# Clustered attention with a gated output block, one core: low parts of k and q by accumulating transfers, key tiles of two more pairs summed ahead of TensorE

## The chip, the cores and the metric

One core of one Trainium2 chip. The metric is the time of one execution on the device in microseconds (us), the median of several runs. An engine works through its own queue of instructions in order; engines wait for each other by semaphores. Names of engines: PE is TensorE, DVE is VectorE, ACT is ScalarE, POOL is GpSimd, SP is SyncE, which issues transfers and computes nothing.

## The reference

For 4 batches of 8 heads (32 heads), 768 positions and head size 64. A query attends only to keys whose nearest of 16 centroids is the same as its own. The result of all heads is the input of a gated block: a causal convolution of 5 taps makes a gate, a 512 by 512 projection makes values, and their product goes through a second projection.

```python
q_assign = np.argmax(np.einsum('bhsd,hcd->bhsc', q_n, c_n), axis=-1)
k_assign = np.argmax(np.einsum('bhsd,hcd->bhsc', k_n, c_n), axis=-1)
mask = q_assign[:, :, :, None] == k_assign[:, :, None, :]
scores = np.where(mask, scale * np.matmul(q, k.transpose(0, 1, 3, 2)), -1e9)
attn = np.exp(scores - max); attn = attn / (np.sum(attn, axis=-1, keepdims=True) + 1e-09)
x = np.matmul(attn, v)          # (B, S, H*D)
gate = 1.0 / (1.0 + np.exp(-causal_conv5(x, conv_w)))
return (gate * (x @ w_val)) @ w_out
```

## The kernel before

The 32 heads form 16 pairs. For each head and each of its 6 tiles of 128 keys, `qk` (L573) makes a 128 by 768 tile of scores in PSUM, keys on the partitions: four matmuls of 384 columns. The products keep fp32 accuracy although the operands are rounded to fp32r, because each of q and k is split into a rounded value and a low part, value minus rounded value. A head has four operands of 128 x 768: x1 holds in its 64 upper rows the low part of k and in its 64 lower rows k rounded; y1 holds q rounded, twice; x2 holds k rounded and under it 16 rows of cluster masks; y2 the low part of q and the masks of q. L580 multiplies x1 by y1, L585 adds x2 by y2.

How the operands come about (L505 to L530): `load_head` (L401) loads k^T and q^T twice each, for the two halves of the partitions, into a ring of three `raw` tiles, through SP's queue. ScalarE makes x2 (`prep_x2`) and y1 (`prep_y1`) by a copy that rounds (`scaled`, L217), then VectorE makes x1 (`prep_x1`) and y2 (`prep_y2`) by subtracting them from the raw values (`both`, L213). The operands have two buffers of each kind, so those of head h can't be written before the last `qk` of head h-2. `prep_mask` copies the mask rows in by transfers from SP.

After `qk`, VectorE takes a row maximum of the first tile (`rowmax`, L599), ScalarE writes the exponentials of every tile into `pt` (`expo`, L608), and TensorE multiplies them with the values (`av`, L725). The denominators are sums over all 6 key tiles. `GROUPS` (L849) says how. With `LG`, VectorE adds the 6 tiles of a head into one tile `ad` (`add_p`, five additions per head) and TensorE sums that over its partitions with one group of matmuls per pair (`sum_p`, L651, four matmuls into four 32-column strips). With `EG`, VectorE adds nothing, and TensorE does such a group for each of the 6 tiles. Before, pairs 1, 2 and 3 have `EG`, the other 13 have `LG`.

The gated block of batch b runs in between the heads of later batches: `scale_x`, `post_x` (high part), `post_xl` (low part), `post_conv` (L754, L756), `sigm`, then `val` (L800), `val_gate`, `val_hi` (L816), `val_lo`, `proj` (L831), `proj_out` (L837), `proj_store`. Weights are split the same way once (`load_w0` to `load_w3`).

The order on every engine is written out by hand: `PLAN` (L1076) lists the operations by number, 2,039 entries; a letter says which engine takes an operation that may go on either, and a number after a point says which buffer it gets. `w` entries are idle matmuls (`warm`, L562) on a tile of zeros. The operations and what they wait for are declared from L887 on (`Op`, with the engines allowed: P TensorE, V VectorE, A ScalarE, G GpSimd, S the queue of SP).

Of the kernel before, what the change touches and what calls it, by code (L numbers as in the profile page):

```python
# [8 lines left out]
F32 = mybir.dt.float32  # L9
# [145 lines left out]
def kernel(  # L155
# [91 lines left out]
    G.memset(qsc[0:D], 1.0)  # L247

# [559 lines left out]
    def val_hi(b, ch, m):  # L808
# [7 lines left out]
        S.activation(hs[b, ch][0][m], gate[:, m, ch * HALF:(ch + 1) * HALF], AF.Copy)  # L816
# [29 lines left out]
    EG = [(0,), (1,), (2,), (3,), (4,), (5,)]  # L846
    LG = [(0, 1, 2, 3, 4, 5)]
    NEG = NP
    GROUPS = [EG if 0 < p < NEG else LG for p in range(NPAIR)]  # L849
# [7 lines left out]
    RING = {"sp": 2, "raw": 3, "sraw": 4, "vt": 2, "rr": 2, "rs": 1, "lr": 1, "ob": 2, "oht": 1, "st": 2}  # L857
# [33 lines left out]
    for n, (h, t) in enumerate(tiles):  # L891
        QK[n] = Op("QK", "P", qk, h, t, after=[QK.get(n - 1)], take="sp")
        if t == 0:
            RM[n] = Op("RM", "V", rowmax, h, t, after=[QK[n]]).frees(QK[n])
        EX[n] = Op("EX", "A", expo, h, t, after=[QK[n], RM[slot[h, 0]]], take="pt").frees(QK[n])
# [42 lines left out]
    for g in range(1, len(groups)):  # L938
# [29 lines left out]
    for p in range(NPAIR):  # L968
        n0, n1 = slot[2 * p, 0], slot[2 * p + 1, 0]
        WT = Op("WT", "P", weigh, p, 0, after=[RM[n0], RM[n1]], take="acc")  # L970
        WM = Op("WM", "V", weigh, p, 1, after=[WT]).frees(WT)
        WC = Op("WE", "A", weigh, p, 2, after=[WM])
        VS[p] = [Op("VS", "A", weigh_v, p, e, after=[WC] + [LV[p]] * (p > 0)) for e in range(2)]
        for j in range(NT):
# [35 lines left out]
    for n, w in enumerate(chunks):  # L1010
# [4 lines left out]
        for j in range(3):  # L1015
            o = Op("W3", "V" if j else "A", load_w3, *w, j, after=[o])
# [5 lines left out]
    for b in range(B):  # L1022
        last = b == B - 1
        for p in range(NP * b, NP * b + NP):
            split = p % NP == NP - 1 or p == NPAIR - 2
            for hf in (0, 1) if split else (None,):
# [9 lines left out]
                PX = Op("PX", "A", post_x, p, *c, after=src + warx)  # L1036
# [12 lines left out]
        for ch in range(2):  # L1049
            for m in range(NC):  # L1050
# [10 lines left out]
                VH[b, ch, m] = Op("VH", "A", val_hi, b, ch, m, after=[VO[b, ch, m]] + war + ([AVK[NPAIR - 1, e, NT - 1] for e in range(2)] if last else []))  # L1061
# [15 lines left out]
        553 0 552 546 969 1 3 548 547 551 559A 560 2.0 558A w35.0 6 555V 550 557V 4.1 7.2 9 12 549 556V 10 11.3 5.0  # L1077
        984.0 985 13.4 986 987 554V w11.2 15 16.5 14.1 740.2 741 988 18 742 743 21 561 752 753 754 744 989.0 8 755
# [3 lines left out]
        772.2 50 51.5 998 999 773 774 1494 1000 776 1009.3 1010 1407V 1011 52 54 53.6 1016.2 783 576 775 55.0 575 1408  # L1082
        56 57.3 1013 58 59.7 1004 1005 577 1019 1022 1012 578 60 62 579 1418V 1409 778 1410 1411 61.8 1419 1420 1025
# [207 lines left out]
```

## Time and profile before

| what | value |
| --- | --- |
| median of 3 runs | 473.2 us (471.87 to 474.07) |
| the profiled execution | 473.45 us |
| its span, first to last instruction | 471.7 us |
| PE busy | 460.9 us, 98% |
| DVE busy | 405.2 us, 86% |
| ACT busy | 333.8 us, 71% |
| POOL busy | 5.3 us, 1% |
| transfers | 63.77 MB, 135 GB/s on average |

Busy is the time in which at least one instruction of the engine is under way. Matmuls overlap: one of 384 columns is listed with some 340 ns, but the next starts about 175 ns after it. So what a matmul costs is read from the starts in the timeline, not from its listed duration.

### The profile page before, as it was taken

The page shows a single profiled execution, that of the slowest core. Times are in us where ns is not written, and L with a number is a line of the kernel's source. Part 1 is how long each engine was busy: PE and PEld are TensorE (multiplying, and loading weights), DVE is VectorE, ACT ScalarE, POOL GpSimd, SP SyncE. Part 2 cuts the span into 40 slices and gives each one's busy share as a digit, 9 for nine tenths or more (in the row PEclk, how much of TensorE's full clock was granted, in tenths as well). Part 3 has the DMA queues.
Part 4 walks back from the last instruction along what each step waited for, and adds up shares of the span by engine and source line. Part 5 has one row for each costly group of instructions (what it writes and reads, how often), then busy time and mean ns, then how long its engine had stood idle before and what let it go on. Part 6 is the DMA issues. An engine that isn't in the chain of part 4 may idle for free. (4 is left out here: it accounts for less than half of the span.)

```text
span 471.7 us, 7756 instructions
## 1 busy us (share of the span) xinstructions
PE 460.9 (98%) x2782; PEld 328.3 (70%) x2782; DVE 405.2 (86%) x690; ACT 333.8 (71%) x489; POOL 5.3 (1%) x35
## 2 busy tenths in 40 slices
PE   8999999999999999999999999999999999999986
PEld 5655564657767777766587696758677896757965
DVE  4997889999999999999999898999987596798550
ACT  6868787977897676986887576878868664655232
POOL 3000000000000000000000000000000000000000
PEclk9999999999999999999999999999999999999999
DMA  7757777575464554656545454636533531110012
GB/s 200 194 167 191 204 210 198 152 209 153 129 187 140 158 133 134 173 190 168 162 114 123 114 165 105 163 97 182 132 106 100 142 95 45 52 59 24 1 47 92
DMA packets 35270, 63.77 MB, mean 135 GB/s; under 512 B 9756, under 2 KB 18332, under 8 KB 35228
## 3 DMA queue, kind: packets, MB, share of 16 engines
q1 hardware_dynamic: 35228, 63.24, 49.1%
q8 instruction: 23, 0.38, 0.3%
q14 instruction: 19, 0.16, 0.1%
HBM read 53.79 MB, written 6.38 MB: 128 GB/s over the span
## 5 line engine op out<-in xcount | busy, mean ns | idle before, releaser
L608 ACT ACTIVATE pt<-sp,sp 128x768 f32<-128x768 f32 x192 | 166.7, 897 | 63.8 <-PE sp L585 39.2
L725 PE MATMUL acc<-pt,vt 128*64 128x384 f32 x768 | 130.7, 490 | 0.5 <-ACT lr L658 0.5
L580 PE MATMUL sp<-op,op 128*128 128x384 f32 x372 | 100.7, 352 | 1.6 <-ACT pt L608 1.4
L213 DVE TENSOR_TENSOR ad<-ad,pt 128x768 f32<-128x768 f32 x104 | 98.2, 951 | 4.5 <-ACT pt L608 1.8
L725 PEld LDWEIGHTS acc<-pt,vt 128*64 128x64 f32 x768 | 52.4, 137 | 68.8 <-issue 63.2
L585 PE MATMUL sp<-op,op 80*128 80x384 f32 (+1 forms) x372 | 95.7, 338 | 0.0
L580 PEld LDWEIGHTS sp<-op,op 128*128 128x128 f32 x372 | 64.7, 188 | 26.4 <-issue 11.6
L756 DVE SCALAR_TENSOR_TENSOR gate<-xr,cw,gate 128x768 f32<-128x768 f32 (+1 forms) x84 | 68.0, 816 | 3.7 <-ACT gate L217 3.0
L585 PEld LDWEIGHTS sp<-op,op 80*128 80x128 f32 (+1 forms) x372 | 68.0, 189 | 0.0
L213 DVE TENSOR_TENSOR op<-raw,op 128x768 fp32r<-128x768 f32 (+3 forms) x64 | 58.5, 919 | 1.4 <-ACT op L217 1.3
L831 PE MATMUL acc<-wh_o,h 128*128 128x512 f32 x144 | 52.7, 403 | 0.0
L800 PE MATMUL acc<-xh,wh_v 128*128 128x384 f32 x112 | 38.6, 344 | 0.0
L800 PE MATMUL acc<-xh,wl_v 128*128 128x384 f32 x112 | 37.8, 337 | 0.0
L800 PE MATMUL acc<-xl,wh_v 128*128 128x384 f32 x112 | 37.7, 337 | 0.0
L831 PEld LDWEIGHTS acc<-wh_o,h 128*128 128x128 f32 x144 | 27.1, 188 | 4.6
L217 ACT ACTIVATE op<-raw 128x768 fp32r<-128x768 f32 x31 | 26.0, 838 | 5.9 <-DMA raw<-qT 4.6
L217 ACT ACTIVATE op<-raw,qsc 128x768 fp32r<-128x768 f32 x31 | 28.9, 932 | 1.2 <-DMA raw<-kT 0.6
L831 PE MATMUL acc<-wl_o,h 128*128 128x512 f32 x72 | 28.4, 395 | 0.0
L213 DVE TENSOR_TENSOR ad<-pt,pt 128x768 f32<-128x768 f32 x26 | 24.5, 944 | 2.3 <-ACT pt L608 2.2
L816 ACT ACTIVATE h<-gate 128x384 fp32r<-128x384 f32 x28 | 14.1, 517 | 12.7 <-DVE gate L806 10.1
L837 ACT ACTIVATE ob<-acc 128x512 f32<-128x512 f32 (+1 forms) x22 | 12.6, 574 | 14.7 <-PE acc L831 13.9
L800 PEld LDWEIGHTS acc<-xh,wl_v 128*128 128x128 f32 x112 | 21.2, 189 | 0.1
(159 smaller groups left out, 526.0 us busy)
## 6 DMA issues: line engine op xcount, KB each, us to landing
raw<-kT SPq DMA_DIRECT2D x62, 192.0 KB, 4.1
raw<-qT SPq DMA_DIRECT2D x62, 192.0 KB, 3.9
sraw<-kT SPq DMA_DIRECT2D x32, 192.0 KB, 2.9
sraw<-qT SPq DMA_DIRECT2D x32, 192.0 KB, 3.6
vt<-v SPq DMA_DIRECT2D x16, 384.0 KB
out_dram<-ob SPq DMA_DIRECT2D x23, 256.0 KB, 2.3
rs<-rr SPq DMA_DIRECT2D x30, 192.0 KB, 4.3
op<-oht SPq DMA_DIRECT2D x56, 48.0 KB, 2.3
```

Of the source, the lines that this page charges most:

```text
L213: (V if on[0] == "V" else G).tensor_tensor(out_, a, b, op=op)
L217: S.activation(out_, in_, AF.Copy, scale=x)
L580: PE.matmul(sp[:, hf, 0:HALF], x1[:, ts_], y1[:, hf * HALF:(hf + 1) * HALF], start=True, stop=False)
L585: PE.matmul(sp[:, hf, 0:HALF], x2[0:KR, ts_], y2[0:KR, hf * HALF:(hf + 1) * HALF], start=False, stop=True)
L608: S.activation(o.rearrange("p (a b) -> p a b", a=2), sp[:, :, 0:HALF], AF.Exp, bias=shift[h], scale=QS)
L725: PE.matmul(acc[e * D:(e + 1) * D, 0:HALF], vt[:, j, e * D:(e + 1) * D], pts[2 * p + e, j][:, hf * HALF:(hf + 1) * HALF], start=(j == 0), ...
L756: V.scalar_tensor_tensor(g, xr[:, k + c0:k + c1], cw[:, ct, k:k + 1], g, op0=ALU.mult, op1=ALU.add)
L800: PE.matmul(macc["v", b, ch, m][:, 0:HALF], a[:, kt, ms], x[:, kt, cs], start=(kt == 0 and i == 0), stop=(kt == NC - 1 and i == 2))
L816: S.activation(hs[b, ch][0][m], gate[:, m, ch * HALF:(ch + 1) * HALF], AF.Copy)
L831: PE.matmul(macc[b, ch, t, c0][:, 0:c1 - c0], x[kt][:, ts_], a[:, kt, c0:c1], start=(kt == 0 and i == 0), stop=(kt == NC - 1 and i == 2))
L837: S.activation(ob[:, 0:c1 - c0], acc[:, 0:c1 - c0], AF.Copy)
```

## The change

It makes the low parts of heads 2 to 31 in another way. For x1, `prep_xn` writes -(k rounded) into the upper rows and k rounded into the lower ones, by one rounding copy scaled by the column `sign`; then `prep_xa` issues from GpSimd a transfer of the 64 rows of k^T from DRAM that adds to what is there, which leaves k minus its rounded value. `prep_yn` and `prep_ya` do the same for y2. The subtractions on VectorE (`prep_x1`, `prep_y2`) are left for heads 0 and 1 only. Each of the four rounding copies (X2, Y1, XN, YN) may run on ScalarE or VectorE, and so may `post_x`, `val_hi` and the first step of `load_w3`; on VectorE `scaled` is now a tensor_scalar. x2 is now written only in its 64 rows of k, so the mask transfer waits for the last `qk` of head h-2 and no more for x1.

`GROUPS` keeps `EG` for pair 1 alone. Pairs 2 and 3 get `LG`: their key tiles are added by VectorE, 20 additions, and summed by one group on TensorE per pair. A few small buffers get rings that are checked, and `PLAN` is written anew (2,110 entries; `w` entries 28, 15 and 11 in place of 35 and 11).

```diff
@@ scaled
         else:
-            G.tensor_scalar(out_, in_, x, 0.0, op0=ALU.mult, op1=ALU.add)
+            V.tensor_scalar(out_, in_, x, None, op0=ALU.mult)
@@ constants
+    sign = const.tile([P, 1], F32, name="sign")
+    G.memset(sign, 1.0)
+    G.memset(sign[0:D], -1.0)
@@ operands
-        return ring(op_p, 2, [P, SQ], F32R, f"op{i}_")
+        return op_p.tile([P, SQ], F32R, name=f"op{i}_{h % 2}", bufs=1)
 
     def prep_x2(h):
 
-        x2 = operand(h, 1)
-        scaled(x2, raws["q", h], qsc)
-        ops.setdefault(h, [None] * 4)[1] = x2
+        dst = ops.setdefault(h, [None] * 4)
+        if dst[1] is None:
+            dst[1] = operand(h, 1)
+        if h == 1:
+            scaled(dst[1], raws["q", h], qsc)
+        else:
+            scaled(dst[1][0:D], raws["q", h][0:D], 1.0)
+
+    def prep_xn(h):
+
+        x1 = ops.setdefault(h, [None] * 4)[0] = operand(h, 0)
+        scaled(x1, raws["q", h], sign)
+
+    def prep_xa(h):
+
+        G.dma_start(out=ops[h][0][0:D], in_=kT[h], accum_op=ALU.add)
+
+    def prep_yn(h):
+
+        if ops.setdefault(h, [None] * 4)[3] is None:
+            ops[h][3] = operand(h, 3)
+        scaled(ops[h][3][0:D], raws["k", h][0:D], -1.0)
+
+    def prep_ya(h):
+
+        G.dma_start(out=ops[h][3][0:D], in_=qT[h], accum_op=ALU.add)
@@ val_hi
-        S.activation(hs[b, ch][0][m], gate[:, m, ch * HALF:(ch + 1) * HALF], AF.Copy)
+        scaled(hs[b, ch][0][m], gate[:, m, ch * HALF:(ch + 1) * HALF], 1.0)
@@ sums
-    GROUPS = [EG if 0 < p < NEG else LG for p in range(NPAIR)]
+    GROUPS = [EG if p == 1 else LG for p in range(NPAIR)]
@@ operations of a head
-        X2 = Op("X2", "A", prep_x2, h, after=[LQ] + war)
-        Y1 = Op("Y1", "A", prep_y1, h, after=[LK] + war)
-        X1 = Op("X1", "V", prep_x1, h, after=[X2]).frees(LQ)
-        Y2 = Op("Y2", "V", prep_y2, h, 0, SQ, after=[Y1]).frees(LK)
-        ready[h] = [X1, Y2]
+        X2 = Op("X2", "AV", prep_x2, h, after=[LQ] + war).frees(LQ)
+        Y1 = Op("Y1", "AV", prep_y1, h, after=[LK] + war).frees(LK)
+        XN = Op("XN", "AV", prep_xn, h, after=[LQ] + war).frees(LQ)
+        YN = Op("YN", "AV", prep_yn, h, after=[LK] + war).frees(LK)
+        XA = Op("XA", "G", prep_xa, h, after=[XN])
+        YA = Op("YA", "G", prep_ya, h, after=[YN])
+        ready[h] = [X2, Y1, XA, YA]
@@ masks
-                    war = ready[h][:1] if j == 0 else [last_qk[h - 2]]
+                    war = [last_qk[h - 2]]
@@ either engine
-            o = Op("W3", "V" if j else "A", load_w3, *w, j, after=[o])
+            o = Op("W3", "V" if j else "AV", load_w3, *w, j, after=[o])
-                PX = Op("PX", "A", post_x, p, *c, after=src + warx)
+                PX = Op("PX", "AV", post_x, p, *c, after=src + warx)
@@ PLAN
-        553 0 552 546 969 1 3 548 547 551 559A 560 2.0 558A w35.0 6 555V 550 557V 4.1 7.2 9 12 549 556V 10 11.3 5.0
...
```

TensorE at the sums of pair 3, before. `pt` are the exponentials of one key tile, `wt` the weights that sum over the partitions, `acc` the PSUM bank; the odd and the even head of the pair alternate, and each two rows come twice, for the two halves of 384 columns:

```order
L585 MATMUL sp_1285<-op_0_1076,op_0_1094 128x384 x2
L651 MATMUL acc_1296<-pt_1197,wt_1276 32x384
L651 MATMUL acc_1296<-pt_1072,wt_1276 32x384
...
L651 MATMUL acc_1296<-pt_1242,wt_1276 32x384
L651 MATMUL acc_1296<-pt_1118,wt_1276 32x384
...
L651 MATMUL acc_1296<-pt_1290,wt_1276 32x384
L651 MATMUL acc_1296<-pt_1173,wt_1276 32x384
...
L457 MATMUL acc_1335<-sraw_1184,cenT 32x384
```

The same place after the change (L606 and L611 are `qk`, L677 is `sum_p`, `ad` the added tile of a head):

```order
L611 MATMUL sp_1370<-op_0_1197,op_0_1253 128x384 x2
L677 MATMUL acc_1387<-ad_1264,wt_1274 32x384
L677 MATMUL acc_1387<-ad_1209,wt_1274 32x384
...
L606 MATMUL sp_1392<-op_0_1257,op_0_1199 128x384 x2
L611 MATMUL sp_1392<-op_0_1197,op_0_1253 128x384 x2
```

Twenty-four rows became four; pair 2 changes in the same way.

ScalarE around the operands of head 10, before (`op_1_1440` is y1, `op_1_1460` x2; `pt` rows are exponentials of head 9):

```order
L608 ACTIVATE pt_1431<-sp_1416,sp_1351 128x768 [waits PE_49]
L217 ACTIVATE op_1_1440<-raw_1407 128x768 [waits DMAHW3_49,DMAHW2_49,PE_49]
L339 ACTIVATE h_638<-h_638 128x512 [waits DMAHW7_49]
L217 ACTIVATE op_1_1460<-raw_1316,qsc 128x768 [waits DMAHW4_49,PE_49]
L608 ACTIVATE pt_1467<-sp_1433,sp_1351 128x768 [waits PE_49]
```

and VectorE, where the two low parts of that head are made:

```order
L213 TENSOR_TENSOR op_1_1490<-raw_1316,op_1_1460 128x768 [waits DMAHW4_49,DMAHW3_49,Activation_49]
L343 TENSOR_SCALAR h_638<-h_638 128x512 [waits DVE_49]
L344 TENSOR_SCALAR h_638<-h_638 128x512 [waits DMAHW7_49]
L741 TENSOR_TENSOR xr_123<-acc_1366,rs_1454 128x384 [waits DMAHW6_49,DMAHW5_49,PE_49]
L213 TENSOR_TENSOR op_1_1457<-raw_1407,op_1_1440 64x768 [waits DMAHW2_49]
```

ScalarE around the operands of head 10 after the change (`op_0_1430` is x1, scaled by `sign`; `op_0_1474` x2, `op_0_1484` y2 negated, `op_0_1504` y1):

```order
L217 ACTIVATE op_0_1430<-raw_1427,sign 128x768 [waits DMAHW1_49,DMAHW0_49,DMASW4_49]
L634 ACTIVATE pt_1442<-sp_1434,sp_1328 128x768 [waits DVE_49,PE_49]
L217 ACTIVATE xh<-xr_130 128x768
L217 ACTIVATE op_0_1474<-raw_1427 64x768 [waits DMAHW4_49]
L217 ACTIVATE op_0_1484<-raw_1457 64x768 [waits DMAHW4_49,DMAHW3_49,DMASW5_49]
L217 ACTIVATE op_0_1504<-raw_1457 128x768 [waits DMAHW5_49]
L634 ACTIVATE pt_1506<-sp_1478,sp_1328 128x768 [waits PE_49]
L634 ACTIVATE pt_1523<-sp_1494,sp_1328 128x768 [waits PE_49,Activation_49]
L634 ACTIVATE pt_1526<-sp_1514,sp_1328 128x768 [waits PE_49]
L634 ACTIVATE pt_1547<-sp_1528,sp_1328 128x768 [waits PE_49,Activation_49]
```

and GpSimd, whose queue had nothing between the start and the last pair (first a transfer of head 9, then the two of head 10, then one of head 11):

```order
L525 DMA op_1_1315<-kT 64x768 [waits DMASW2_49,Activation_49]
L525 DMA op_0_1430<-kT 64x768 [waits DMASW4_49,PE_49,Activation_49]
L535 DMA op_0_1484<-qT 64x768 [waits DMASW5_49,DMAHW3_49,PE_49,Activation_49]
L525 DMA op_1_1586<-kT 64x768 [waits DMASW7_49,PE_49,Activation_49]
```

The two subtractions left VectorE; ScalarE has four copies of head 10 where it had two, and the two transfers wait for ScalarE and for earlier users of the same buffer.

## Rows read from the trace of the kernel before

**Rows 1.** The page: busy engines; TensorE's busy share in 40 slices, in tenths.
```profile
PE 460.9 (98%) x2782; PEld 328.3 (70%) x2782; DVE 405.2 (86%) x690; ACT 333.8 (71%) x489; POOL 5.3 (1%) x35
PE   8999999999999999999999999999999999999986
```
**Rows 2.** Stretches: us, busy time (instructions) of each engine, PEclk, DMA share, GB/s.
```profile
30.00:60.00 30.00, 28.73 (x187) 15.83 (x184) 25.36 (x54) 22.60 (x32) 0.00 (x0) 1.00 0.74 197
60.00:90.00 30.00, 30.00 (x199) 17.02 (x199) 27.57 (x55) 24.36 (x34) 0.00 (x0) 1.00 0.77 203
160.00:200.00 40.00, 40.00 (x232) 29.00 (x231) 39.12 (x68) 31.62 (x48) 0.00 (x0) 1.00 0.53 139
200.00:240.00 40.00, 40.00 (x233) 26.48 (x232) 38.98 (x59) 31.11 (x46) 0.00 (x0) 1.00 0.57 164
```
**Rows 3.** Who waited for whom, PE: us in total, times, longest.
```profile
PE sp L580 <- ACT pt L608: 1.4, 2, 0.8
PE acc L651 <- DVE ad L213: 0.3, 1, 0.3
```
**Rows 4.** Timeline of PE: start us, us until the last end, instruction, count.
```profile
13.26 2.13 PE L566 MATMUL acc<-idle 128*128 128x128 bf16 x35
15.20 0.59 PE L580 MATMUL sp<-pt,pt 128*128 128x384 f32 x2
...
39.94 0.85 PE L651 MATMUL acc<-ad,wt 128*32 128x384 f32 x8
40.72 0.62 PE L580 MATMUL sp<-op,op 128*128 128x384 f32 x2
...
74.34 2.79 PE L651 MATMUL acc<-pt,wt 128*32 128x384 f32 x32
76.94 0.83 PE L457 MATMUL acc<-sraw,cenT 128*32 128x384 f32 x8
77.59 1.47 PE L651 MATMUL acc<-pt,wt 128*32 128x384 f32 x16
78.99 0.61 PE L580 MATMUL sp<-op,op 128*128 128x384 f32 x2
...
96.60 4.08 PE L651 MATMUL acc<-pt,wt 128*32 128x384 f32 x48
100.50 0.83 PE L457 MATMUL acc<-sraw,cenT 128*32 128x384 f32 x8
```
**Rows 5.** Groups of DVE: line, operation, out<-in, count | busy, mean ns | idle before.
```profile
L213 DVE TENSOR_TENSOR ad<-ad,pt 128x768 f32<-128x768 f32 x104 | 98.2, 951 | 4.5 <-ACT pt L608 1.8
L213 DVE TENSOR_TENSOR op<-raw,op 128x768 fp32r<-128x768 f32 x30 | 28.4, 945 | 0.0
L213 DVE TENSOR_TENSOR op<-raw,op 64x768 fp32r<-64x768 f32 x30 | 28.2, 941 | 1.4 <-ACT op L217 1.3
L213 DVE TENSOR_TENSOR h<-h,wh_o 128x512 f32<-128x512 f32 x4 | 2.7, 681 | 0.0
L343 DVE TENSOR_SCALAR h<-h 128x512 int32<-128x512 int32 x6 | 2.5, 420 | 0.1
```
**Rows 6.** Groups of ACT, same columns.
```profile
L608 ACT ACTIVATE pt<-sp,sp 128x768 f32<-128x768 f32 x192 | 166.7, 897 | 63.8 <-PE sp L585 39.2 <-DVE sp L603 15.1 <-PE acc L725 8.8
L217 ACT ACTIVATE op<-raw,qsc 128x768 fp32r<-128x768 f32 x31 | 28.9, 932 | 1.2 <-DMA raw<-kT 0.6 <-PE sp L585 0.4
L217 ACT ACTIVATE op<-raw 128x768 fp32r<-128x768 f32 x31 | 26.0, 838 | 5.9 <-DMA raw<-qT 4.6 <-PE sp L580 1.4
```
**Rows 7.** The tile raw: its transfers of 192 KB, whole run and 30 to 90 us.
```profile
DMA to landing us min/median/max: 3.2/4.0/6.5
...
DMA to landing us min/median/max: 3.3/4.9/6.5
```
**Rows 8.** The page: the SP queue's transfers, MB, share of 16 engines' span.
```profile
q1 hardware_dynamic: 35228, 63.24, 49.1%
```
**Rows 9.** Who waited for whom: GpSimd's one long wait.
```profile
POOL st L704 <- DVE rc L671: 422.0, 1, 422.0
```

More of the change, by code (lines that the diff above doesn't have):

```diff
@@ L845 @@
     NAD = 2
-    EG = [(0,), (1,), (2,), (3,), (4,), (5,)]
     LG = [(0, 1, 2, 3, 4, 5)]
-    NEG = NP
-    GROUPS = [EG if 0 < p < NEG else LG for p in range(NPAIR)]
+    EG = [(j,) for j in range(NT)]
+    GROUPS = [EG if p == 1 else LG for p in range(NPAIR)]
     NTILE = NH * NT
@@ L893 @@
         if t == 0:
-            RM[n] = Op("RM", "V", rowmax, h, t, after=[QK[n]]).frees(QK[n])
-        EX[n] = Op("EX", "A", expo, h, t, after=[QK[n], RM[slot[h, 0]]], take="pt").frees(QK[n])
+            RM[n] = Op("RM", "V", rowmax, h, t, after=[QK[n]], take=None if h % 2 else "shift").frees(QK[n])
+        EX[n] = Op("EX", "A", expo, h, t, after=[QK[n], RM[slot[h, 0]]], take="pt").frees(QK[n], RM[slot[h - h % 2, 0]])
         for g, js in enumerate(GROUPS[h // 2]):
@@ L970 @@
         WT = Op("WT", "P", weigh, p, 0, after=[RM[n0], RM[n1]], take="acc")
-        WM = Op("WM", "V", weigh, p, 1, after=[WT]).frees(WT)
-        WC = Op("WE", "A", weigh, p, 2, after=[WM])
-        VS[p] = [Op("VS", "A", weigh_v, p, e, after=[WC] + [LV[p]] * (p > 0)) for e in range(2)]
+        WM = Op("WM", "V", weigh, p, 1, after=[WT]).frees(WT, RM[n0])
+        WC = Op("WE", "A", weigh, p, 2, after=[WM], take="wt")
+        VS[p] = [Op("VS", "A", weigh_v, p, e, after=[WC] + [LV[p]] * (p > 0)).frees(WC) for e in range(2)]
         for j in range(NT):
@@ L982 @@
                     LL[p, g] = Op("LL", "P", sum_p, p, g, after=[LL.get((p, g - 1)), WC] + ad, take=None if g else "acc")
-                    LL[p, g].frees(*([AD[h, g, 1] for h in (2 * p, 2 * p + 1)] if len(js) > 1 else ex))
+                    LL[p, g].frees(WC, *([AD[h, g, 1] for h in (2 * p, 2 * p + 1)] if len(js) > 1 else ex))
         prev.frees(LV[p])
@@ L987 @@
             LC = dma("LC", sum_spread, p, after=[LE]).frees(LE)
-            RC = Op("RC", "V", recip, p, after=[LC])
-            RR = dma("RR", recip_row, p, after=[RC], take="rr")
+            RC = Op("RC", "V", recip, p, after=[LC], take="rc")
+            RR = dma("RR", recip_row, p, after=[RC], take="rr").frees(RC)
             RS = dma("RS", recip_rows, p, after=[RR], take="rs").frees(RR)
@@ L994 @@
             LT = Op("RT", "P", sum_t, p, after=[LE], take="acc").frees(LE)
-            RQ = Op("RC", "V", recip_q, p, after=[LT]).frees(LT)
+            RQ = Op("RC", "V", recip_q, p, after=[LT], take="rc").frees(LT)
             late.append(LT)
@@ L998 @@
                 AVO[p, hf] = Op("AO", "A", av_out, p, hf, after=[AVK[p, hf, NT - 1]]).frees(AVK[p, hf, 0])
-                RB = Op("RB", "G", recip_b, p, hf, after=[RQ], take="st")
+                RB = Op("RB", "G", recip_b, p, hf, after=[RQ], take="st").frees(RQ)
                 RT = Op("RT", "P", recip_t, p, hf, after=[RB], take="acc").frees(RB)
@@ L1060 @@
                 war = ([] if last else [PJ[b, 0, t, NC - 1] for t in range(TPH)]) if ch else [PJ[b - 1, 1, t, NC - 1] for t in range(TPH)] if b else [use[0], use[1]]
-                VH[b, ch, m] = Op("VH", "A", val_hi, b, ch, m, after=[VO[b, ch, m]] + war + ([AVK[NPAIR - 1, e, NT - 1] for e in range(2)] if last else []))
+                VH[b, ch, m] = Op("VH", "AV", val_hi, b, ch, m, after=[VO[b, ch, m]] + war + ([AVK[NPAIR - 1, e, NT - 1] for e in range(2)] if last else []))
                 VL[b, ch, m] = Op("VL", "V", val_lo, b, ch, m, after=[VH[b, ch, m]])
@@ new lines @@
+        130 1149.2 1150.0 1151 1152 1153 1154 1155 1141 1521A 888 643 1575 137 905 906 901 133 1143 140 902 1522 907
+        1523 1142 138.8 1524 1574 141.11 1161.3 143 146 1162 144.0 1576 147.6 139.0 903.1 904 1605.3 889 1525 149
+        150.4 644 648A 642 650 152 153 154.10 908 1163 1164 909.1 1526 1581A 645 910 1052 1577 1578 1156 1157 1158
+        1159 646A 1160 155 1582 649A 651 925 1169.1 142 1579 158 1606 1165 647A 156.3 157.1 1170 145 161 890 1166
+        159.9 1168 162.5 164 1607 891 167 1167 1612.1 165.12 652 653 1613 1171 1173 168.1 660 170 173 1172 1174.0
@@ L1168 @@
+        2091 2103 2013 2080 2081A 2082 2104 2105 2106 2014V 1983 2020 2084 2085 2021A 2086 2026 2033 2092 1999 2000
+        2015 2022 1984 2027 2034 2035V 2093 2043.0 2037.2 2094 2044 2028A 2087 2029 2038 2036 2045 2046 2088 2039 2040
+        2047 2048 2049.1 2050 2041 2051 2052 2042 2053 2095.2 2096 2054 2097 2098 2099 2100
     """
```

102 lines of the change are left out of this document (90 added, 12 removed), and 79 rows, old and new, of the table PLAN.

## The prediction

> **What bounds the kernel now.** I read the page first: TensorE is busy for 98% of the span, VectorE for 86%, and the slices of TensorE are nines from the second to the last but one [rows 1]. Then the stretches: from 60 to 90 and from 160 to 240 us TensorE has no gap, at full granted clock, while VectorE reaches 39.12 of 40 us from 160 to 200 [rows 2]. VectorE is thus nearly full, yet it holds up nothing: the list of waits has 0.3 us of TensorE for VectorE's added tiles and 1.4 us for the exponentials [rows 3]. So the time is the length of TensorE's queue. A part that shortens that queue is worth its whole length, anything on another engine nothing until it makes TensorE wait. The reader should check one thing before going on: busy matmuls overlap, so the price of a group on TensorE is the distance from its first start to the next instruction's start.
>
> **TensorE's queue.** Per pair with single-tile sums there are six groups, 48 matmul instructions (an fp32 matmul is two). Pair 2: 74.34 to 76.94 and 77.59 to 78.99, 2.60 + 1.40 = 4.00 us. Pair 3: 96.60 to 100.50, 3.90 us [rows 4]. Both go: -7.90 us. Each gets one group on added tiles, which stands alone between other matmuls: 39.94 to 40.72, 0.78 us [rows 4], so +1.56 us for two. The idle matmuls rise from 46 to 54 in the plan; 35 of them took 13.26 to 15.20, 0.055 us each [rows 4], so +0.44 us, if they do not fall into waiting time. All other matmuls are the same in number and shape. Sum on TensorE: -7.90 + 1.56 + 0.44 = -5.9 us.
>
> **VectorE.** Sixty subtractions of 943 ns go, 56.6 us (28.4 + 28.2); 20 additions of 951 ns come, 19.0 us [rows 5]. The rounding copies that the new plan gives to VectorE are 37 of 768 columns, 15 of 384 and 5 of 512. No row has such a copy with an fp32r result; the bounds are a tensor_scalar with one input, 420 ns for 512 columns, and a tensor_tensor with two, 681 ns [rows 5]. Scaled by columns that is 0.63 us to 0.944 us for 768, and about 30 to 47 us in all. VectorE ends between 8 us lower and 9 us higher than its 405; I take the one-input row, since the copy has one input. All of it lies beside TensorE's queue. That cover is thin where 20 additions enter early, but there the subtractions of the same heads leave; the cost is 0 as long as the sums of pairs 2 and 3 are not late.
>
> **ScalarE.** It loses 62 copies of 838 and 932 ns [rows 6] and has 89 of nearly the same widths, 27 more, about +22 us; nine `val_hi` copies, ten of `post_x` and five of weights leave it, narrower or as wide, so up to 20 us. From 333.8 it comes to between 336 and 356 us, at most 75%: hidden, as its waits for scores in TensorE's queue are 39.2 us on the exponentials alone [rows 6].
>
> **Transfers, and the wait that is added.** This is the unknown. Sixty transfers of 192 KB on GpSimd's queue are new, 11.8 MB. At the price of the existing ones (63.24 MB for 49.1% of 16 engines [rows 8]) that is 9% more; if an addition reads, adds and writes back at twice the price, 18%. From 30 to 90 us the share is already 0.74 and 0.77 [rows 2]. About 14 of the new transfers, 2.75 MB, fall there: by the same price 10 us of 60, so 0.92; at twice the price over 1. SP's queue gets no new transfer. GpSimd issues nothing else between the start and the last pair, where it now sits idle for 422 us [rows 9], so only the transfers queue behind each other there.
>
> Behind each transfer stands `qk` of its head, and behind that all of TensorE's queue. How long is the slack? From the order: after ScalarE's last negated copy of head 10 come y1 and four exponentials, of which the last frees the PSUM tile that `qk` of head 10 needs: 0.838 + 4 x 0.897 = 4.4 us [rows 6]. Counting so for all heads (on TensorE's rows where the copy is on VectorE), the shortest slack is 4.4 us, heads 3, 7, 15, 18, 20, 28 and 30 have 5.0 to 5.5, five more up to 6.4 (2, 5, 24, 25, 29), the rest more. (For heads 12 and 17 ScalarE's count gives less, but the exponential before the copy does not hold it back, so TensorE's rows ahead of `qk` count there, and these give more.)
>
> How long the addition takes from issue to landing no row shows. Bounds: a plain load of the same 192 KB lands after 4.0 us (median; 3.2 at best), 4.9 from 30 to 90 us; the slowest took 6.5 [rows 7]. I take 4.9, the median where the load is highest, for it is nearest in size and place. Against the slacks it costs 0.5 us, at head 10. At 3.2 or 4.0 it costs nothing. At 6.5 it costs what is missing at thirteen heads, whose slacks add up to 72.0 us: 13 x 6.5 - 72.0 = 12.5 us.
>
> The Trainium skill has a rule that speaks against the change, SBUF — State Buffer, section "SBUF: two separate sides": a transfer issued from GpSimd has its descriptors written by GpSimd, which is locked out while VectorE runs a one-input copy on both of its ports; its advice is to issue from another queue. No row here shows it, since GpSimd issues no transfer in the trace. By it the time is that of the second rival below, 470.8 us; by the rows of the loads alone 468.0.
>
> **The sum.** The profiled execution took 473.45 us, 0.25 above the median of 473.2. 473.45 - 5.9 + 0.5 = 468.0 us; against the median 467.8. I forecast **468.0**, 1.1% faster. Its own range is 465 to 470.5: down where idle matmuls and waits at the start fall away, up where two or three heads wait for a microsecond. A measurement here tells about 0.5%, 2.4 us, from no change.
>
> **Rivals.**
> - *The addition lands late.* Each head's first `qk` waits, and nothing on TensorE can overtake it. The point at which it decides is where the missing slack equals 5.9 us: at 5.9 us from copy to landing the sum over heads is 6.4 (head 10 alone 1.5). At 6.5 us the time is 473.45 - 5.9 + 12.5 = 480; at 8 us nearly all heads miss and some 40 us come on top, but ScalarE's gaps (29% idle) lengthen the slack, so I hold 480 for the middle of this case. For it: the transfer reads its destination too, the early share is near full, GpSimd's own part is unseen. Against it: loads in the trace rarely need more than 4.9, and most slacks are above 5. Slower. 22%.
> - *GpSimd's issue waits for VectorE.* If each transfer is held until the instruction on VectorE ends, up to one copy of 0.63 us, 4.9 becomes 5.5 and the missing slack 3.2 us: 473.45 - 5.9 + 3.2 = 470.8. For it: VectorE is up to 98% busy in the middle [rows 2]. Against it: only some 57 instructions there are copies, so most transfers meet none. 12%, at the edge of no change.
> - *VectorE becomes the bound.* If the copies cost 0.944 us, VectorE has 414 us, and the added tiles of pairs 2 and 3 arrive late; what TensorE saved it spends waiting, and the time stays at 473 to 475. For it: 0.98 busy from 160 to 200. Against it: the 57 us leave just there, where no additions are added. 8%.
> - The forecast: 58%.
>
> **Chances and range.** Faster by over 0.5%: the forecast and a little of the second rival, 0.60. Within: the rest of the second and most of the third, 0.15. Slower: the first and what is left, 0.25. The range goes from 464.5 (-7.90 alone, and one microsecond of the waits at the start) to 482 (the late landing at 6.5 us with VectorE at its upper price); about 1 in 10 lies above and less below.
>
> **What would show it.** Right: TensorE without gaps from 60 us on, in pairs 2 and 3 one group of 8 matmul instructions each on `ad`, at about 0.78 us, in place of 48; issue to landing of the additions under 5 us; VectorE below 400. Wrong: waits of the first `qk` of a head for a transfer on x1 or y2, 0.5 us and more at many heads, growing where the DMA share is near 1; or waits of `sum_p` for `ad`. A tensor_scalar of 768 columns above 0.9 us would break the VectorE term, a missing wait with no gain would break the first view, that TensorE's queue is the time.

## The result, and the profile after

The change makes the kernel slower: 478.94 us median (478.79 to 480.09, 4 runs) against 473.58 (471.87 to 474.07, 4 runs) for the kernel before, a ratio of 1.0125 with an interval of 1.0094 to 1.0156. The forecast was 468.0. The time is inside the range and its sign is wrong. All times below are medians over the runs left when one slow run each of e2 (484.06 us) and e4 (478.81 us) is set aside.

The page of the profiled execution (478.79 us, span 477.1), first the engines, then the share of the transfer engines in 40 slices, then the two queues that carry data (q1 is SP's, q0 GpSimd's):

```profile
PE 459.9 (96%) x2710; PEld 326.4 (68%) x2710; DVE 395.2 (83%) x703; ACT 341.8 (72%) x496; POOL 55.7 (12%) x97
DMA  7599799889958577756658385676657573111002
q1 hardware_dynamic: 35228, 63.24, 46.7%
q0 software_dynamic: 4800, 11.80, 15.7%
```

TensorE has 72 matmul instructions fewer than in [rows 1] and is listed as busy for almost as long, in a longer span. VectorE, ScalarE and GpSimd have room; what is new is 15.7% of the transfer engines for 11.80 MB, 1.33% for a megabyte, where q1 pays 0.74%. The stretches of [rows 2], after:

```profile
30.00:60.00 30.00, 28.44 (x183) 15.95 (x184) 25.96 (x53) 22.55 (x33) 4.84 (x6) 1.00 0.86 209
60.00:90.00 30.00, 29.07 (x164) 16.84 (x162) 27.31 (x48) 27.12 (x38) 4.48 (x6) 1.00 0.97 254
160.00:200.00 40.00, 39.79 (x223) 29.98 (x221) 37.83 (x72) 32.22 (x47) 6.35 (x7) 1.00 0.74 185
200.00:240.00 40.00, 37.93 (x222) 23.91 (x224) 35.40 (x55) 28.87 (x43) 4.06 (x5) 1.00 0.63 157
```

From 60 to 90 and from 200 to 240 us TensorE had no gap before and now has 0.9 and 2.1 us, at the same full granted clock. Over 30 to 400 us its idle time, the stretch less its busy time, is 9.8 us; in the kernel before it is 1.6. (Idle understates what is lost: a gap shows only behind the listed end of the last matmul.) The DMA share of the second row, 0.97, is the highest here. It is not a ceiling: it sums the times of all packets, and e2 and e3 reach 1.06 and 1.08 in the same stretch. Who waited for whom after (us in total, times, longest):

```profile
DVE xr L767 <- DMA rs<-rr: 10.3, 9, 2.4
ACT op L217 <- DMA raw<-qT: 6.8, 6, 1.9
PEld acc L460 <- DMA sraw<-qT: 3.5, 4, 1.2
PE sp L611 <- DMA op<-qT: 3.2, 6, 1.2
PE acc L677 <- DVE ad L213: 1.9, 1, 1.9
PE acc L460 <- DVE xr L767: 1.5, 2, 1.0
PE sp L606 <- DMA op<-kT: 0.8, 1, 0.8
```

The same view of the kernel before, for the first three:

```profile
ACT op L217 <- DMA raw<-qT: 4.6, 2, 3.4
PEld acc L457 <- DMA sraw<-qT: 1.0, 2, 0.8
DVE xr L741 <- DMA rs<-rr: 0.9, 2, 0.5
```

One kind of wait is new and one has grown. TensorE waits at `qk` for an addition (`op<-qT`, `op<-kT`), 4.0 us in all. And transfers that the change does not touch come late: the wait for the reciprocals of `scale_x` (`rs<-rr`) goes from 0.9 to 10.3 us, and those for the tiles of the cluster search (`sraw`) and for the raw tiles grow too. The wait of TensorE for `xr` and for `ad` can be the end of such a chain: a late `rs` holds VectorE, and VectorE's next results hold TensorE. The longest one, from the timelines (in brackets the engine's idle time before the row):

```profile
236.24 0.56 DVE L767 TENSOR_TENSOR xr<-acc,rs 128x384 f32<-128x384 f32 x1 [2.38 <-DMA rs<-rr]
236.71 2.81 DVE L213 TENSOR_TENSOR ad<-ad,pt 128x768 f32<-128x768 f32 x3
239.67 0.85 PE L677 MATMUL acc<-ad,wt 128*32 128x384 f32 x8 [1.91 <-DVE ad L213]
```

Either kind could be the cause; the experiments have to tell which.

The rows of the terms, after. The timeline of TensorE at the sums of pair 2, that took 4.00 us in [rows 4]:

```profile
85.20 0.85 PE L677 MATMUL acc<-ad,wt 128*32 128x384 f32 x8
85.99 0.34 PE L491 MATMUL acc<-om,first 128*128 128x384 bf16 x1
```

VectorE's groups (mean ns in the last figure before the second bar), that answer [rows 5]:

```profile
L213 DVE TENSOR_TENSOR ad<-ad,pt 128x768 f32<-128x768 f32 x120 | 113.4, 951 | 3.4 <-ACT pt L634 0.4
L219 DVE TENSOR_SCALAR op<-raw 64x768 fp32r<-64x768 f32 x22 | 11.9, 547 | 8.7 <-PE sp L611 7.8 <-DMA raw<-qT 0.5 <-DMA op<-oht 0.3
L219 DVE TENSOR_SCALAR op<-raw,sign 128x768 fp32r<-128x768 f32 x7 | 4.3, 608 | 1.6 <-DMA raw<-kT 1.5
```

And the additions, from issue to landing (the tile `op`) and one of their two lines, with min, median and max of GpSimd's own part in ns:

```profile
DMA to landing us min/median/max: 3.4/5.2/7.7
L525 POOL DMA_DIRECT2D op<-kT x30: 806/806/1299, 27.7 to 401.9; - x30
```

### The profile page after: what moved, and what is told of

Read it like the earlier page. It is cut to its first block, busy times and chain, and to the rows that moved or that the text cites. A ratio compares the mean times of both kernels' runs of the same rounds, so it can differ in the third digit from the quotient of the medians.

```text
span 477.1 us, 7796 instructions
## 1 busy us (share of the span) xinstructions
PE 459.9 (96%) x2710; PEld 326.4 (68%) x2710; DVE 395.2 (83%) x703; ACT 341.8 (72%) x496; POOL 55.7 (12%) x97
## 3 DMA queue, kind: packets, MB, share of 16 engines
q0 software_dynamic: 4800, 11.80, 15.7%
## 5 line engine op out<-in xcount | busy, mean ns | idle before, releaser
L213 DVE TENSOR_TENSOR ad<-ad,pt 128x768 f32<-128x768 f32 x120 | 113.4, 951 | 3.4 <-ACT pt L634 0.4
L606 PE MATMUL sp<-op,op 128*128 128x384 f32 x372 | 101.7, 354 | 1.8 <-ACT pt L634 0.9
L611 PE MATMUL sp<-op,op 80*128 80x384 f32 (+1 forms) x372 | 96.5, 340 | 4.0 <-DMA op<-qT 3.2
L606 PEld LDWEIGHTS sp<-op,op 128*128 128x128 f32 x372 | 64.2, 189 | 26.2 <-ACT pt L634 11.5
L611 PEld LDWEIGHTS sp<-op,op 80*128 80x128 f32 (+1 forms) x372 | 67.4, 189 | 6.7 <-DMA op<-qT 5.1
L217 ACT ACTIVATE op<-raw 64x768 fp32r<-64x768 f32 (+1 forms) x65 | 53.6, 837 | 7.1 <-DMA raw<-qT 6.8
L857 PE MATMUL acc<-wh_o,h 128*128 128x512 f32 x144 | 51.2, 400 | 0.0
L525 POOL DMA_DIRECT2D op<-kT x30 | 25.9, 863 | 215.4 <-ACT op L217 151.0
L535 POOL DMA_DIRECT2D op<-qT x30 | 27.5, 918 | 130.0 <-ACT op L217 71.2
L213 DVE TENSOR_TENSOR ad<-pt,pt 128x768 f32<-128x768 f32 x30 | 28.4, 950 | 2.8 <-PE acc L677 2.0
L625 DVE TENSOR_REDUCE nm<-sp 128x1 f32<-128x384 f32 x32 | 17.6, 551 | 8.4 <-PE sp L611 8.3
L767 DVE TENSOR_TENSOR xr<-acc,rs 128x384 f32<-128x384 f32 x30 | 15.9, 551 | 10.3 <-DMA rs<-rr 10.3
L863 ACT ACTIVATE ob<-acc 128x512 f32<-128x512 f32 (+1 forms) x22 | 12.5, 573 | 15.2 <-PE acc L857 11.8
```

The costliest lines, as they stand in the source:

```text
L213: (V if on[0] == "V" else G).tensor_tensor(out_, a, b, op=op)
L525: G.dma_start(out=ops[h][0][0:D], in_=kT[h], accum_op=ALU.add)
L535: G.dma_start(out=ops[h][3][0:D], in_=qT[h], accum_op=ALU.add)
L606: PE.matmul(sp[:, hf, 0:HALF], x1[:, ts_], y1[:, hf * HALF:(hf + 1) * HALF], start=True, stop=False)
L611: PE.matmul(sp[:, hf, 0:HALF], x2[0:KR, ts_], y2[0:KR, hf * HALF:(hf + 1) * HALF], start=False, stop=True)
L625: V.tensor_reduce(out=nm, in_=spt[h, t][:, 0, 0:HALF], op=ALU.max, axis=AX.X, negate=True)
```

## The experiments

All eleven start from the changed kernel; the cuts of code below show one place of each edit. The table has the time, the ratio to the kernel before in the same batch, the share of the engines that GpSimd's queue took, and TensorE's idle time from 30 to 400 us (the stretch's length less its busy time, in the profiled execution).

| run | us | ratio (95% interval) | q0 share | PE idle |
| --- | --- | --- | --- | --- |
| kernel before | 473.6 | | 0 | 1.6 |
| changed kernel | 478.94 | 1.0125 (1.0094 to 1.0156) | 15.7% | 9.8 |
| e1 no transfers | 465.1 | 0.9815 (0.9782 to 0.9849) | 0 | 0.3 |
| e2 additions into spare tiles | 477.91 | 1.0103 (1.0028 to 1.0177) | 16.1% | 10.8 |
| e3 plain copies | 471.55 | 0.9938 (0.9910 to 0.9966) | 11.8% | 3.2 |
| e6 additions by GpSimd itself | 542.07 | 1.1434 (1.1384 to 1.1484) | 0 | 43.9 |
| e4 one raw load | 474.73 | 1.0013 (0.9978 to 1.0049) | 15.9% | 6.7 |
| e5 one raw load, whole | 488.97 | 1.0321 (1.0296 to 1.0345) | 15.8% | 17.3 |
| e7 late heads only | 471.06 | 0.9943 (0.9920 to 0.9966) | 10.7% | 5.9 |
| e8 early heads only | 472.26 | 0.9968 (0.9949 to 0.9986) | 5.3% | 4.9 |
| e9 half width | 468.35 | 0.9868 (0.9823 to 0.9913) | 8.5% | 3.3 |
| e11 e2 and e4 together | 472.94 | 0.9987 (0.9952 to 1.0022) | 15.9% | 5.6 |
| e12 additions read SBUF | 492.02 | 1.0383 (1.0325 to 1.0440) | 18.3% | 17.3 |

### e1: the change without its transfers

```diff
-        G.dma_start(out=ops[h][0][0:D], in_=kT[h], accum_op=ALU.add)
+        return
```

and the same in `prep_ya`.

> The changed kernel without its sixty accumulating transfers (the low parts of heads 2 to 31 are left as minus the rounded values); order, copies and sums as changed. Theory A, late landing: the first matmuls of a head waited for the additions, some 5 us in all in the trace of the changed kernel; with these alone gone the time is 478.9 - 5 = 474. Theory B, crowding: the 11.8 MB also delay other transfers (the spread reciprocals, the loads); A and B together give back all that TensorE's queue lost, 467 to 469 us, as the sum of the prediction has it (473.5 - 5.9 = 467.6). Theory C, the new order itself is worse by its other waits: 474 or more, with VectorE's waits for the spread reciprocals still near 10 us.

465.1 us, 8.5 below the kernel before. TensorE's stretch from 60 to 90 us is full again, and the wait for `rs` is gone:

```profile
60.00:90.00 30.00, 30.00 (x174) 18.09 (x170) 29.29 (x54) 29.05 (x42) 0.00 (x0) 1.00 0.75 201
DVE xr L767 <- DMA rs<-rr: 0.4, 1, 0.4
```

So the rest of the change does what was forecast of it, and more; the sixty transfers cost 13.8 us (478.9 - 465.1).

### e2: the same transfers, but nobody waits for them

```diff
-        G.dma_start(out=ops[h][0][0:D], in_=kT[h], accum_op=ALU.add)
+        G.tensor_copy(mark, ops[h][0][0:1, 0:1].bitcast(F32))
+        G.dma_start(out=away[0][0:D], in_=kT[h], accum_op=ALU.add)
```

> The same sixty accumulating transfers, issued at the same places after the same copies (a tiny copy on GpSimd waits for them), but into two spare tiles that nobody reads, so no matmul waits for them (the low parts are left as minus the rounded values). Theory A (late landing alone): 474, like the kernel without transfers. Theory B (crowding of the other transfers alone): 478 to 479, like the changed kernel, and the one without transfers is at 467 to 469. Both at work: in between, 472 to 475, with the distance to the kernel without transfers being the crowding.

477.91 us, over a spread of 476.58 to 481.73: what is won by taking the wait for the landing away is 1 us, inside the scatter. (Part of this run's loss is its own: the spare tiles are zeroed at the start, where TensorE is busy for 26.4 of the first 30 us in place of 26.8.) What waits now:

```profile
DVE xr L773 <- DMA rs<-rr: 11.9, 8, 2.4
ACT op L217 <- DMA raw<-qT: 9.0, 7, 2.6
PE acc L683 <- DVE ad L213: 2.8, 3, 2.1
```

The late landing alone is not the cause: 12.8 of the 13.8 us are there without any wait for it. The other transfers come late with or without it, and where TensorE doesn't wait for an addition, it waits at the next late thing.

### e3: plain copies of the same bytes

```diff
-        G.dma_start(out=ops[h][0][0:D], in_=kT[h], accum_op=ALU.add)
+        G.dma_start(out=ops[h][0][0:D], in_=kT[h])
```

> The sixty transfers from GpSimd as plain copies that do not accumulate (raw values stand where low parts should). If reading and adding at the destination is what makes them late and heavy, issue to landing falls from 5.2 us (median) to the 4 us of a plain load, their share of the transfer engines from 15.7% towards 9%, and the time by 3 to 5 us, to 474 to 476. If it is the way by GpSimd, or the bytes as such, landing and time stay: 478 to 479.

471.55 us, 2.5 us below the forecast for plain copies. The same 4,800 packets and 11.80 MB cost 6.5 us as plain copies and 13.8 as additions. The page of this run, queue and issue, its wait for `rs`, and its stretch from 60 to 90 us:

```profile
q0 software_dynamic: 4800, 11.80, 11.8%
L525 POOL DMA_DIRECT2D op<-kT x30 | 16.0, 532 | 222.2 <-ACT op L217 157.3
DVE xr L767 <- DMA rs<-rr: 4.7, 5, 1.6
60.00:90.00 30.00, 29.68 (x168) 16.89 (x168) 29.33 (x53) 28.03 (x40) 3.06 (x6) 1.00 1.08 245
```

An addition holds the transfer engines longer: 0.157 x 477.1 x 16 / 4800 = 250 ns for a packet, against 0.118 x 467.8 x 16 / 4800 = 184 ns (the shares of both are rounded, and 960 of the 4,800 packets carry 4 bytes; the 3,840 of 3,072 bytes take 307 and 216 ns on average). In the trace's packet records the fastest twentieth of the packets of 3,072 bytes takes up to 252 ns as an addition, 135 ns as a plain copy from the same queue and 121 ns in SP's queue: undisturbed, an addition has 1.9 times the price. GpSimd's issue is also longer, 0.81 us in place of 0.51 where it is undisturbed.

The last row is a warning: the share of the stretch is higher here than with additions, 1.08 against 0.97, and TensorE idles for 0.3 us in place of 0.9. The total share of the engines does not say by itself what is lost.

### e6: GpSimd adds, no transfer

```diff
-        G.dma_start(out=ops[h][0][0:D], in_=kT[h], accum_op=ALU.add)
+        x1 = ops[h][0][0:D]
+        G.tensor_tensor(x1, raws["q", h][0:D], x1.bitcast(F32), op=ALU.add)
```

> The additions as instructions on GpSimd (raw value plus minus the rounded one, 64 x 768) in place of the transfers, in the same places of its queue. A subtraction of 64 x 256 took 0.715 us there, so one takes some 2.1 us by columns, 60 of them 128 us on an engine that is else idle, and the result is there 2 to 3 us after the copy and not 5 to 6. Theories A and B: no late landing and no crowding, 467 to 470. If GpSimd and VectorE hold each other up on two-input instructions, additions on VectorE grow from 0.95 us, and the time stays above 473. Theory C: 474 or more.

542.07 us, far worse. Groups of VectorE and GpSimd:

```profile
L213 DVE TENSOR_TENSOR ad<-ad,pt 128x768 f32<-128x768 f32 x120 | 143.1, 1199 | 4.2 <-ACT pt L636 0.9 <-ACT xh L217 0.5
L526 POOL TENSOR_TENSOR op<-raw,op 64x768 fp32r<-64x768 f32 x30 | 66.3, 2212 | 211.3 <-ACT op L217 153.2
L219 DVE TENSOR_SCALAR op<-raw 64x768 fp32r<-64x768 f32 x22 | 16.3, 747 | 7.8 <-PE sp L613 7.2 <-DMA raw<-qT 0.6
```

GpSimd takes 2.2 us for an addition of 64 rows, and VectorE's instructions grow on average: 951 to 1,199 ns for the added tiles, 547 to 747 for the copies; VectorE has 469 us in place of 395. TensorE's granted clock was 0.951 over the span, 0.998 in the changed kernel, which lengthens the run further. So this run decides nothing between the theories. The Trainium skill, page "SBUF — State Buffer", section "SBUF: two separate sides", says that a GpSimd instruction that reads SBUF and a VectorE instruction with two SBUF inputs lock each other out of a shared pair of ports for their whole length; the 26% on `ad` agree with it.

### e4: the additions as they are, less other traffic

The raw tiles are kept from head to head, and from head 4 on only their upper rows are loaded:

```diff
-        for c in range(2):
+        for c in range(1 if h > 3 else 2):
```

> The changed kernel with all sixty accumulating transfers, but from head 4 on each raw tile is loaded for its 64 upper rows only (the three raw tiles are kept, so that the lower rows hold what an earlier head left): 56 loads of 192 KB, 11.0 MB, fall out of SP's queue, and no instruction of an engine changes. Left out: the lower rows of x1 and y1 are of another head. Theory A (the additions crowd the other transfers where the engines' share is near 1): the total share falls from 62% of the span to about 55%, between the plain copies' run (62%) and the run without transfers (49%); TensorE's idle time from 30 to 400 us falls from 9.8 us to 1 to 3 us, and the time is 466 to 470 us. Theory B (an accumulating transfer is dear by itself: GpSimd's longer issue, its later landing, its hold on a transfer engine, whatever else runs): the sixty are all still there, and the time stays at 475 to 480 us.

474.73 us, over a wide spread (470.62 to 477.63 in nine runs): 4.2 us back of 13.8. The engines' share fell to 56%, below that of the plain copies (63%), and the time is 3.2 us above theirs. Theory A in its simple form, that the total share near 1 is what hurts, falls with this; theory B is not right either. One event of the profiled execution shows a part of what is left. Landing of the additions, then from the timeline SP's load of weights, GpSimd's issue, and TensorE, and last the stretch behind it:

```profile
DMA to landing us min/median/max: 3.3/4.8/9.7
69.23 0.58 SPq L327 DMA_DIRECT2D xl<-w_val  x1
69.31 0.91 POOL L537 DMA_DIRECT2D op<-qT  x1
79.10 0.79 PE L613 MATMUL sp<-op,op 80*128 80x384 f32 x2 [2.01 <-DMA op<-qT]
78.00:82.00 4.00, 2.90 (x10) 2.07 (x12) 2.01 (x4) 1.30 (x2) 1.03 (x2) 0.67 0.78 173
```

An addition issued beside a weight load of 512 KB lands 9.7 us later, and TensorE idles for 2.0 us. That looks like a collision of transfers in a stretch, not a share of the span; no run takes the weight load away. The gap costs more than its length: right behind it TensorE's granted clock falls from full (2.4 GHz) to half (1.2 GHz) for a while, a mean of 0.67 in the last row, where the changed kernel's rows have 1.00. This bears on the spread: the five runs with a granted clock of 0.998 or more have a median of 472.91 us, the four with 0.992 to 0.995 one of 476.08.

### e5: a whole version with that saving

From head 2 on only the upper rows are loaded, and the lower halves of x1 and y1 come from the same 64 raw rows by a second copy into the lower partitions, right behind the first (for x1):

```diff
-        scaled(x1, raws["q", h], sign)
+        scaled(x1[0:D], raws["q", h][0:D], -1.0)
+        scaled(x1[D:2 * D], raws["q", h][0:D], 1.0)
```

> A whole version of the change with less traffic: from head 2 on each raw tile is loaded for its 64 upper rows only (60 loads, 11.8 MB, fewer), and the lower halves of x1 and y1 are made from the same 64 rows by a second rounding copy that writes the lower partitions, right behind the first on the same engine: 49 more copies on ScalarE (0.84 us each, 41 us, to about 381 us) and 11 on VectorE (0.55 us, 6 us). Theory A: the crowding goes, and what is left is ScalarE at about 81% of the span; 467 to 473 us, and below the kernel before if the copies find ScalarE's gaps. Theory B: as now or worse, 478 to 485 us. If ScalarE's fuller queue makes the scores' PSUM tiles come free later, TensorE waits for pt in the list of waits, and the time can be above 475 under either theory; then the waits for raw, rs and sraw still tell: near those of the run without transfers under A, unchanged under B.

488.97 us. ScalarE rose to 382 us (78%), and it is late for TensorE; the wait for `rs` fell as under A:

```profile
PE sp L611 <- ACT pt L639: 11.7, 21, 1.3
DVE xr L772 <- DMA rs<-rr: 2.4, 3, 1.3
```

The copies stand in front of exponentials that TensorE needs next. An engine at 78% is not free at each place of a fixed order.

### e7 and e8: where the additions stand

```diff
-        G.dma_start(out=ops[h][0][0:D], in_=kT[h], accum_op=ALU.add)
+        if h > 11:
+            G.dma_start(out=ops[h][0][0:D], in_=kT[h], accum_op=ALU.add)
```

and the same in `prep_ya`, for e7 (heads 12 to 31); `h < 12` for e8 (heads 2 to 11).

> The changed kernel with the accumulating transfers of heads 12 to 31 only (40 of 60); the low parts of heads 2 to 11 stay minus the rounded values. The loss of the sixty is 478.9 - 465.1 = 13.8 us. Theory A: it lies where the share is near 1, which is in the first 160 us (TensorE's idle time of the changed kernel is 5.5 us from 30 to 160 us and 4.3 us from 160 to 400 us), so the forty late ones cost 13.8 x 4.3 / 9.8 = 6 us: 471 us (469 to 472.5). Theory B: every accumulating transfer costs the same, 0.23 us: 465.1 + 40 x 0.23 = 474.3 us (473.5 to 476).

> The counterpart: the accumulating transfers of heads 2 to 11 only (20 of 60). Theory A: 465.1 + 13.8 x 5.5 / 9.8 = 472.8 us (471 to 474.5), more than the forty late ones. Theory B: 465.1 + 20 x 0.23 = 469.7 us (468.5 to 470.5), half of the late ones.

471.06 and 472.26 us. Forty late additions cost 6.0 us, twenty early ones 7.2; together 13.2 of the 13.8. Each early one costs 0.36 us, each late one 0.15: B, with one price for all, is out. Two stretches of e7, then the same of e8:

```profile
60.00:90.00 30.00, 30.00 (x171) 18.09 (x170) 29.24 (x54) 28.97 (x42) 0.00 (x0) 1.00 0.72 200
240.00:280.00 40.00, 37.62 (x215) 29.32 (x214) 31.83 (x58) 28.28 (x41) 6.15 (x8) 1.00 0.69 172
```

```profile
60.00:90.00 30.00, 28.64 (x160) 16.55 (x158) 26.89 (x49) 27.36 (x38) 4.41 (x6) 1.00 0.97 257
240.00:280.00 40.00, 40.00 (x236) 33.05 (x235) 34.36 (x63) 31.87 (x46) 0.00 (x0) 1.00 0.50 140
```

TensorE loses where the additions run and hardly anywhere else: 1.4 of 30 us at a share of 0.97, and 2.4 of 40 us at 0.69. Theory A gave the right times, but the loss does not need a share near 1.

### e9: half the width

```diff
-        G.dma_start(out=ops[h][0][0:D], in_=kT[h], accum_op=ALU.add)
+        G.dma_start(out=ops[h][0][0:D, 0:HALF], in_=kT[h, :, 0:HALF], accum_op=ALU.add)
```

> The changed kernel with sixty accumulating transfers of 384 columns in place of 768 (96 KB each, 5.9 MB in all); the low parts of columns 384 to 767 stay minus the rounded values. Theory A2 (what an addition costs is the time it holds the transfer engines: the full ones hold them for 15.7% of the span, plain copies of the same bytes for 11.8%): the engines' share falls to about 8%, the loss against the run without transfers halves, 465.1 + 6.9 = 472 us (470 to 473.5). Theory C (each accumulating transfer delays others and its own head as one, by its issue on GpSimd and its latency, whatever its size): 476 to 479 us.

468.35 us: sixty additions of half the width cost 3.3 us, a quarter of the whole. Theory C is out, and A2's 472 us, with the loss in proportion to the hold, is missed by 3.7 us. The hold is what counts (8.5% in place of 15.7%; with e3, the same bytes for 11.8%, it is not the bytes), and the loss grows faster than the hold. GpSimd issues as many transfers as before, and each issue is as long (median 0.81 us), so its issuing is not the price. Nor do the additions slow VectorE's own work: `ad` takes 951 ns in the changed kernel and in e1.

### e11: nobody waits, and less other traffic

e2's and e4's edits in one kernel.

> Two earlier edits together: the sixty accumulating transfers go to two spare tiles that nobody reads (no head waits for a landing), and from head 4 on each raw tile is loaded for its upper rows only (11.0 MB fewer). Left out: the low parts are minus the rounded values, and the lower rows of x1 and y1 are of another head. The light run with the additions in place took 474.9 us, with 3.0 us of waits of TensorE for a landing. If what is left there is the wait for landings (theory D: two costs, crowding and landing, each hidden behind the other when only one is taken away), it falls to 466 to 470 us. If the additions' hold on the transfer engines delays the others even at the lower share (theory A2), it stays at 473 to 476 us.

472.94 us. Against e4 that is 2 us, inside the scatter of both (the intervals overlap), so D is neither shown nor excluded as a small part. Against e2 it is 5.0 us: of the 12.8 us that are left when nobody waits for a landing, two fifths are gone with 11.0 MB of other loads. That part is crowding. The rest, 7.8 us above e1, stays although nobody waits and the share is down, just below the 473 to 476 that A2 expected; some of it is the zeroing at the start (TensorE busy for 26.0 of the first 30 us, 27.3 in e1) and some the granted clock, 0.94 from 30 to 60 us in the profiled execution.

### e12: additions that read SBUF

```diff
-        G.dma_start(out=ops[h][0][0:D], in_=kT[h], accum_op=ALU.add)
+        G.dma_start(out=ops[h][0][0:D], in_=raws["q", h][0:D], accum_op=ALU.add)
```

> The whole change, but the additions read the upper rows of the raw tile in SBUF in place of k^T and q^T in DRAM. The raw tiles are then held until the additions have landed, so the next loads into them start later. If part of an addition's price is the read from DRAM, the software queue's share falls below 15.7% towards the plain copies' 11.8%, and the time comes down by up to the 7.4 us that separate the two (471.5 to 477 us). If the price is the addition itself (read, add and write back at the destination), the share stays, the raw tiles come free later, and the time is 479 to 485 us.

492.02 us, 7 us above the upper forecast. The queue, and the raw tiles that now come free only at the landing:

```profile
q0 software_dynamic: 4800, 11.80, 18.3%
ACT op L217 <- DMA raw<-qT: 15.6, 7, 5.2
```

The share did not fall, and the fastest twentieth of the packets takes 252 ns here too, so the read from DRAM is not what makes an addition dear. The price belongs to adding, whatever the source. The time itself says less, since the later raw tiles are a cost of this edit alone.

## Why the prediction was wrong, point by point

- **TensorE's queue** (-5.9 us) was right. The sum of pair 2 takes 85.20 to 85.99, 0.79 us where 0.78 was taken, and without its transfers the kernel is 8.5 us faster than before. What goes beyond the sum is mostly idle time that the kernel before still had: span less busy time of TensorE is 10.8 us there and 6.9 in e1 (whose profiled execution, 462.83 us, is 2.3 us below its median).
- **VectorE** was right in direction, and its copies still cheaper: 0.547 us for 64 rows, 0.608 for 128 with the column `sign`, where 0.63 to 0.944 was the bound. It ends 10 us lower, 395 us in all, 2 us outside the stated 8 lower to 9 higher. (The upper bound was not what its row gives: 681 ns for 512 columns is 1.02 us for 768; 0.944 is the mean of the subtractions of 768 columns. Nothing hangs on it.) Rival "VectorE becomes the bound": no.
- **ScalarE** was right: 341.8 us, between 336 and 356.
- **GpSimd's issue**: minimum and median of the line shown are both 0.81 us, so most issues waited for nothing while VectorE was busy for 83% of the span. The means of the two lines, 0.86 and 0.92 us, leave some 0.1 us for an issue where that rival took up to 0.63. It has no support here.
- **The step that failed is the transfers' term, "Against the slacks it costs 0.5 us".** It was wrong by 13.3 us, in three ways. First, it took one number, 4.9 us, for a landing that spreads from 3.4 to 7.7 (median 5.2); heads with a slack of 5 to 6 us wait for the upper part of that spread, not for its middle: 4.0 us of idle TensorE. Nor did the slacks hold head by head: the first `qk` waits at heads 3, 7, 11, 17, 20, 22 and 30, three of which (11, 17, 22) the count had above 6.4 us, and not at head 10, which had the least. Second, the price: the text had "twice the price" as a bound, and 18% of the engines by it. Measured it is 15.7%, and 1.9 times the price in the undisturbed packet. The bound was there, and the sum did not use it. Third and largest, the sum asked only who waits for the new transfers. It had the early share at 0.92 to over 1 (measured 0.86 and 0.97) and charged nothing for it. The loads that were there before have no slack counted anywhere in it: `rs`, `sraw`, the raw tiles, the masks, the weights. They come late, and e2 shows that 12.8 of the 13.8 us stay when no head waits for an addition. The early share was only half the warning: the late additions cost 6.0 us in e7, whose stretches behind 120 us have shares of 0.52 to 0.69.
- **The rival "the addition lands late"** came near in time (480) by a mechanism that is at most a part. Its price was the missing slack of the heads; with that wait taken away the time moved by no more than its scatter. That the measured time lies inside the range is luck: its upper part was there for this mechanism. The rival that would have been right, "the additions make other transfers late", was not among them, though its number, the early share, stood in the text.

Shown: the loss is the transfers' (e1); it needs no wait for their landing (e2); it grows with the time that they hold the engines, as the same bytes cost 6.5 us plain and 13.8 added (e3) and half the width costs a quarter (e9); it lies where they run (e7, e8). Argued from the lists of waits, and from no run that takes these waits away: that the late `rs`, raw and `sraw` loads are the path by which it reaches TensorE. Open: why 11.0 MB of other loads less give back only 4.2 us (e4) and 5.0 (e11 against e2). The total share does not rank the losses: 63% with 13.8 us, 63% with 6.5 (e3), 56% with 9.6 (e4). The collision at 69 us suggests that what counts is who is under way at the same moment, and no run here takes single collisions away.

None of the eleven is a whole kernel that beats the one before: e1, e3, e7, e8 and e9, which are faster, leave low parts out. The twenty early additions alone cost 7.2 of the 8.5 us that the rest of the change brings, and VectorE, at 29.3 of 30 us from 60 to 90 us in e1, has little room to make those low parts itself.

## What to carry to other kernels

A transfer that nobody waits for can still cost the time: price a new transfer by how long it holds the engines, then list the loads that share its stretch and what slack each of them has, before asking who waits for the new one. A wait that is removed on a queue with several near-late chains can give nothing back while the crowding behind all of them stays. And when a bound in the text ("over 1") says that a resource is full, it needs a term in the sum, though the share alone is not the price: plain copies at 1.08 cost TensorE less than additions at 0.97.

## What was not expected of the hardware

An accumulating transfer into SBUF holds a transfer engine 252 ns for a packet of 3,072 bytes, a plain copy from the same queue 135 ns, and 139 ns for an accumulating packet of 1,536 (all three where undisturbed): additions run at about half the rate of copies. Reading from SBUF in place of DRAM doesn't lower it (252 ns again, and 18.3% against 15.7%). The Trainium skill, page "DMA: Bandwidth & Descriptors", section "SDMA does more than copy", names add units in line with the data; no run here shows the units themselves, only that adding costs 1.9 times a copy. GpSimd needs 0.81 us to issue one, 0.51 us for a plain copy.
